# Five neighbouring rows on a partition for wq, w1, x and gate_w, and w2's tile zeroed in eight pieces behind the gate

## The chip, the cores and the metric

The kernel runs on one core of a Trainium2 chip. The metric is the time of one execution in device microseconds (us). Lower is better. The core has a matrix engine (PE), a vector engine (DVE), a scalar engine (ACT), GpSimd (POOL) and a synchronisation engine (SP) that here only issues transfers. Sixteen DMA engines move data between device memory and the on-chip memory, which has 128 partitions.

## The reference

The kernel computes the output of a gated mix of two branches for one token (one row x of 640 values), and the gradients of nine inputs. Branch A is attention over a cache of 32 heads, 4096 positions and 128 features a head. Branch B is a dense layer with the Mish activation. All tensors are bf16.

```python
# x: [1,1,640]; k_cache, v_cache: [1,32,4096,128]; wq: [640,4096]; wo: [4096,640]
# w1: [640,1728]; b1: [1728]; w2: [1728,640]; gate_w: [640]
q = (x @ wq).reshape(1, 1, 32, 128).transpose(0, 2, 1, 3)
p = softmax(einsum("bhqd,bhkd->bhqk", q, k_cache) * 128 ** -0.5)
a = einsum("bhqk,bhkd->bhqd", p, v_cache).transpose(0, 2, 1, 3).reshape(1, 1, 4096) @ wo
h = x @ w1 + b1
b = (h * tanh(softplus(h))) @ w2
g = sigmoid((x * gate_w).sum(-1, keepdims=True))
out = g * a + (1 - g) * b
# returned: out and the gradients for x, k_cache, v_cache, wq, wo, w1, b1, w2, gate_w
```

The two caches are 33.6 MB each and are read once. Their gradients are as large and are written once. wq, wo, w1 and w2 (5.2, 5.2, 2.2 and 2.2 MB) are read once, and so are their gradients written. That is 164 MB of traffic in all. Each gradient of a weight is an outer product (the gradient of wq is x times a row), and so is the gradient of each cache head.

## The kernel before, in words

**Heads.** The loop at L758 takes one head after another. A head's K and V tile are [128 partitions, 32 positions, 128 features] with 8192 contiguous bytes on a partition. PE transposes them (L530) and ACT copies the transposed pieces out of PE's accumulators (L539); PE forms the rows of scores (L553), a short chain of DVE, PE and ACT does the softmax (L576 to L608), and DVE writes the two outer products (L613) into a buffer of four (`o_sb`), from which SP stores them (L631). `dv_out` and `dk_out` are these two, and in the last heads they write into the K and V buffers instead. Four K and four V buffers are loaded ahead: behind a head's first store SP issues the loads of the head four later (L809, L810, issuing at L106 and L111).

**Groups.** Four heads make a group. A group needs its slice of wq for the queries (`g_q`, L230) and a tile of wo (transposed at L343) for the gradient that enters each head (`g_do`, L282). wq is loaded for two groups at once (`load_wqp`, L123) into a tile [128, 5, 1024]. When a group is through, its slice of wq is overwritten in place by the gradient (`f_dwq`, L391) and the tile is stored (`f_dwq_st`, L396). The 640 rows of wq lie on 128 partitions, so each partition holds five rows: row r is on partition r mod 128.

**Branch B.** `w1_sb` is [128, 5, 1728] with the same order of rows, loaded at L148 as the last of the first loads; its gradient is written over it (L515) and stored by L822 and L823 in the last but one turn of the loop. `w2_sb` [128, 16, 640] is loaded by POOL through a list of row numbers (`w2_load`, L196, issued in head 0) that leaves 20 of the 128 partitions out; half the tile is set to zero before (L416). The pieces of branch B are worked off a list (`mq`), a few to a head.

**Vectors.** x, grad_out and gate_w come in as five rows of 128 each (L130 to L132, on ACT's queue), fifteen rows in one tile. PE transposes them in one go (L691), so that element c*128+p is on partition p, column c; `cols_bf` and `cols_f` hold the fifteen columns. The first matmul for the queries (L230) needs the columns and the first wq tile. At the end `fin` [128, 15] holds the output and the gradients of x and gate_w as columns; PE transposes it back (L934), ACT copies it (L936) and POOL stores three times five rows (L937 to L939).

**Gate.** z is the sum of x*gate_w, and `g_raw` (L713) the sigmoid of it; `g_all` and `omg_all` scale grad_out for the two branches (L729, L730, L732).

**Order.** Each engine works through its instructions in the order in which they are written; there is no planner. SP's queue holds nearly all the transfers: the first loads (K0, wq, wo, V0, K1, V1, K2, wo, V2, K3, V3, w1), then the stores and loads of each head. ACT's queue holds four small loads at the start, and POOL's the loads of b1 (L418), small moves for branch B, the two transfers of w2 and the last stores. POOL's first work is the identity (L155, L156), small memsets (L209 to L214), the memset of h_sb (L415) and that of w2's half tile (L416), then the loads of b1. DVE's first work is built from the identity; `ident_f` (L165) is what PE's first transposes wait for.

Of the kernel before, what the change touches and what calls it, by code (L numbers as in the profile page):

```python
# [10 lines left out]
F32 = mybir.dt.float32  # L11
BF16 = mybir.dt.bfloat16
# [4 lines left out]
def kernel(  # L17
# [24 lines left out]
    nc = tc.nc  # L42
    P = 128
    _, H, Sk, Dh = A_k_cache.shape
    D = A_x.shape[-1]
# [3 lines left out]
    RC = D // P  # L49
    G = 4  # L50
    NG = H // G
    GD = G * Dh
    FCN = 16
# [14 lines left out]
    dVv = out_3.rearrange("b h (p j) d -> (b h) p j d", p=P)  # L68
    wq_v = A_wq.rearrange("(rc r) c -> r rc c", r=P)
    dwq_v = out_4.rearrange("(rc r) c -> r rc c", r=P)  # L70
    wo4_v = A_wo.rearrange("(g p t) n -> g p t n", p=P, t=4)
    dwo4_v = out_5.rearrange("(g p t) n -> g p t n", p=P, t=4)
    assert G == 4 and NG % 2 == 0
    w1_v = B_w1.rearrange("(rc r) f -> r rc f", r=P)
    dw1_v = out_6.rearrange("(rc r) f -> r rc f", r=P)
    w2_v = B_w2.rearrange("(i fc) n -> i (fc n)", fc=FCN)
    dw2_v = out_8.rearrange("(i fc) n -> i (fc n)", fc=FCN)
    b1_v = B_b1.rearrange("(i fc) -> i fc", fc=FCN)
    db1_row = out_7.rearrange("(o f) -> o f", o=1)
    x_rows = A_x.rearrange("a b (c p) -> (a b c) p", p=P)  # L80
    dy_row = grad_out.rearrange("a b d -> (a b) d")
    dy_rows = grad_out.rearrange("a b (c p) -> (a b c) p", p=P)
    gw_rows = gate_w.rearrange("(c p) -> c p", p=P)
    out0_rows = out_0.rearrange("a b (c p) -> (a b c) p", p=P)
    out1_rows = out_1.rearrange("a b (c p) -> (a b c) p", p=P)
    out9_rows = out_9.rearrange("(c p) -> c p", p=P)

# [40 lines left out]

    vec_rows = const.tile([3 * RC, P], BF16, name="vec_rows")
    nc.scalar.dma_start(vec_rows[0:RC, :], x_rows)  # L130
    nc.scalar.dma_start(vec_rows[RC:2 * RC, :], dy_rows)
    nc.scalar.dma_start(vec_rows[2 * RC:3 * RC, :], gw_rows)  # L132
    mjunk = const.tile([P, F], BF16, name="mjunk")
# [13 lines left out]
    w1_sb = const.tile([P, RC, F], BF16, name="w1_sb")  # L147
    nc.sync.dma_start(w1_sb[:], w1_v)  # L148
    w2_sb = const.tile([P, FCN, D], BF16, name="w2_sb")
# [25 lines left out]
    def grp(shape, dt, name):  # L175
        return grp_ps.tile(shape, dt, name=name, tag="grp")
# [82 lines left out]
    def g_qcol(g):  # L259
        groups[g]["col"] = col_mm(groups[g]["q_row"])  # L260
# [154 lines left out]
    nc.gpsimd.memset(h_sb[:], 0.0)  # L415
    nc.gpsimd.memset(w2_flat[0:P // 2, :].bitcast(F32), 0.0)  # L416
    for a, b, i in SEG:
# [340 lines left out]
    for h in range(H - 1):  # L758
# [211 lines left out]
```

## Time and profile before

| | |
|---|---|
| median of 3 runs | 401.1 us (400.16 to 402.86) |
| the profiled execution | 400.45 us, span 398.5 us, granted PE clock 0.912 |
| PE, DVE, ACT, POOL busy | 305.1, 294.4, 232.8, 18.6 us |
| DMA queue of SP | 159.62 MB in 27312 packets, 96.5% of sixteen engines' span |
| DMA queue of POOL | 4.44 MB in 672 packets, 2.8% |
| moved in all | 164.55 MB, 413 GB/s over the span |

The span runs from the first to the last instruction of the profiled execution; the execution's own time has 1.95 us around it. An engine's busy time is the time in which it worked on an instruction. The DMA share is the mean busy share of the sixteen DMA engines; as packets overlap a little in the records, it can go somewhat over 1. A packet is one contiguous piece that a DMA engine moves.

### The profile page before, as it was taken

How to read it: one execution, taken by the hardware profiler on the slowest of the kernel's cores; microseconds unless marked ns; L12 is line 12 of the kernel's file. 1: busy time of each engine (PE TensorE's matmuls, PEld its weight loads, DVE VectorE, ACT ScalarE, POOL GpSimd, SP SyncE). 2: the span in 40 equal slices, each digit the busy share in tenths (PEclk: the TensorE clock that was granted, in tenths of full speed). 3: DMA queues.
4: the chain of work that ended last, by engine and by line, in shares of the span. 5: the costliest groups of instructions: out<-in, count | busy, mean ns of one | idle time of the engine just before them, and what ended most of it. 6: DMA issues, size and time to landing. Idle time of an engine off the chain costs nothing.

```text
span 398.5 us, 7712 instructions
## 1 busy us (share of the span) xinstructions
PE 305.1 (77%) x2933; PEld 206.1 (52%) x2949; DVE 294.4 (74%) x819; ACT 232.8 (58%) x468; POOL 18.6 (5%) x34
## 2 busy tenths in 40 slices
PE   2979979697898985885888977968797988677540
PEld 1556637464556663553565645645465645455320
DVE  8217728769696875778898986687898986669790
ACT  2466746654667663763566778575678756375320
POOL 8001010000000000000000030000000000010001
PEclk9999999968998998999898999879899899889855
DMA  7999999999999999999999999999999999999996
GB/s 271 424 416 409 401 425 421 424 420 424 423 426 424 422 417 423 426 415 427 424 423 425 422 424 421 426 412 423 427 423 426 423 424 421 423 435 404 406 417 251
DMA packets 28052, 164.55 MB, mean 413 GB/s; under 512 B 2967, under 2 KB 2968, under 8 KB 11416
## 3 DMA queue, kind: packets, MB, share of 16 engines
q1 hardware_dynamic: 27312, 159.62, 96.5%
q0 software_dynamic: 672, 4.44, 2.8%
q8 instruction: 23, 0.38, 0.4%
q14 instruction: 13, 0.11, 0.1%
q10 hardware_dynamic: 32, 0.01, 0.0%
HBM read 82.44 MB, written 82.44 MB: 414 GB/s over the span
## 4 chain that ended last, share of the span: by engine, by line
DMA 46%; DVE 28%; PE 17%; ACT 5%; issue 2%; POOL 0%; POOLq 0%; DVEq 0%; ACTq 0%
DMA out_dram<-o_sb 44%; DVE o_sb L613 10%; PE tr L530 7%; DVE junk L381 4%; DMA out_dram<-Vn 2%; DVE wq_p L391 2%; PE rw L553 2%; PE rw L646 2%; DVE mjunk L510 1%; DVE ident_f L165 1%; PE do_ps L282 1%; ACT do_row L285 1%; DVE Vn L613 1%; PE x L570 1%; ACT rw_sb L564 1%
## 5 line engine op out<-in xcount | busy, mean ns | idle before, releaser
L539 ACT COPY T<-tr 128x512 f32<-128x512 f32 x256 | 137.9, 595 | 54.6 <-PE tr L530 36.6
L613 DVE TENSOR_TENSOR o_sb<-qs_row,ds 128x2048 bf16<-128x2048 bf16 x58 | 70.7, 1218 | 35.5 <-DMA out_dram<-o_sb 35.5
L530 PE MATMUL tr<-ident_f,Vn 128*128 128x128 f32 x512 | 87.3, 306 | 6.8 <-ACT T L539 6.1
L530 PE MATMUL tr<-ident_f,Kn 128*128 128x128 f32 x512 | 85.7, 295 | 7.3 <-DVE ident_f L165 7.3
L530 PEld LDWEIGHTS tr<-ident_f,Vn 128*128 128x128 f32 x512 | 65.3, 158 | 27.9 <-PE tr L530 12.7
L530 PEld LDWEIGHTS tr<-ident_f,Kn 128*128 128x128 f32 x512 | 61.6, 150 | 23.8 <-PE rw L646 13.5
L613 DVE TENSOR_TENSOR o_sb<-do_row,p 128x2048 bf16<-128x2048 bf16 x58 | 69.8, 1246 | 0.0
L564 ACT COPY rw_sb<-rw 128x512 f32<-128x512 f32 x33 | 19.3, 586 | 49.1 <-PE rw L553 47.6
L646 PE MATMUL rw<-Kn,ds 128*4 128x512 bf16 x256 | 36.7, 413 | 3.5 <-DVE ds L608 3.2
L646 PE MATMUL rw<-Vn,p 128*4 128x512 bf16 x256 | 36.7, 413 | 0.0
L582 PE MATMUL mx<-ident_f,m_s 128*128 128x128 f32 x32 | 10.4, 325 | 27.5 <-DVE m_s L578 27.4
L570 PE MATMUL x<-ident_f,rw_sb 128*128 128x128 f32 x132 | 22.1, 291 | 4.6 <-ACT rw_sb L564 1.4
L381 DVE SCALAR_TENSOR_TENSOR junk<-wq_p,dq_bc 128x512 bf16<-128x512 bf16 x35 | 23.9, 684 | 0.0
L553 PE MATMUL rw<-T,qz 128*32 128x512 bf16 x256 | 22.5, 429 | 0.0
L598 PE MATMUL mx<-zd,ones_f 128*128 128x2 f32 x64 | 10.9, 241 | 14.2 <-DVE pj L594 14.0
L399 ACT ACTIVATE wo_g<-da_bc,o 128x640 bf16<-128x640 bf16 x28 | 20.9, 818 | 1.0 <-PE ax_ps L369 1.0
L553 PE MATMUL rw<-T,doz 128*32 128x512 bf16 x256 | 20.7, 400 | 0.8 <-ACT T L539 0.8
L590 ACT ACTIVATE e_bf<-x,negM 128x32 bf16<-128x32 f32 x32 | 9.4, 292 | 20.5 <-DVE dqo L654 20.3
L570 PEld LDWEIGHTS x<-ident_f,rw_sb 128*128 128x128 f32 x132 | 14.1, 143 | 13.5 <-ACT rw_sb L564 13.5
L582 PEld LDWEIGHTS mx<-ident_f,m_s 128*128 128x128 f32 x32 | 4.5, 141 | 32.0 <-DVE m_s L578 31.9
L646 PEld LDWEIGHTS <-ds 128*4 128x4 bf16 x256 | 9.3, 87 | 19.9 <-DVE ds L608 8.2
L598 PEld LDWEIGHTS mx<-zd,ones_f 128*128 128x128 f32 x64 | 10.5, 207 | 17.2 <-DVE pj L594 14.6
(177 smaller groups left out, 381.9 us busy)
## 6 DMA issues: line engine op xcount, KB each, us to landing
out_dram<-o_sb SPq DMA_DIRECT2D x58, 1024.0 KB, 16.2
Kn<-in_A_k_cache_dram SPq DMA_DIRECT2D x32, 1024.0 KB, 16.1
Vn<-in_A_v_cache_dram SPq DMA_DIRECT2D x32, 1024.0 KB, 17.7
wq_p<-in_A_wq_dram SPq DMA_DIRECT2D x4, 1280.0 KB, 14.2
wo_g<-in_A_wo_dram SPq DMA_DIRECT2D x8, 640.0 KB, 17.0
out_dram<-wo_g SPq DMA_DIRECT2D x8, 640.0 KB, 16.4
out_dram<-wq_p SPq DMA_DIRECT2D x4, 1280.0 KB, 10.9
out_dram<-Kn SPq DMA_DIRECT2D x3, 1024.0 KB, 10.0
```

The lines of the kernel that those rows point to most:

```text
L381: nc.vector.scalar_tensor_tensor(jq[:], in0=wqs[g][:, c, :], scalar=1.0, in1=groups[g]["dq_bc"][:], op0=ALU.mult, op1=ALU.mult, accum_out= ...
L399: nc.scalar.activation(wos[g][:, hh, :], da_bc[:], ACT.Copy, scale=groups[g]["o4"][:, hh:hh + 1])
L530: nc.tensor.transpose(tp[:, t, :], words[:, t * P:(t + 1) * P], ident_f[:])
L539: nc.scalar.copy(T[h][:, (3 - c) * (TB // 2):(4 - c) * (TB // 2), :], tp[:])
L553: nc.tensor.matmul(rw[32 * c:32 * (c + 1), :], lhsT=z[:, par, :, :].rearrange("p m u -> p (m u)"), rhs=Tb[:, c, par, :, :], start=first an ...
L564: nc.scalar.copy(rw_sb[h][:].rearrange("p t r -> p (t r)"), rw[:])
L570: nc.tensor.transpose(xs[h][:, 3 - j, :], t[:, j, :], ident_f[:])
L582: nc.tensor.transpose(mx[:, 0:P], dgms.pop(h)[:].to_broadcast([P, P]), ident_f[:])
L590: nc.scalar.activation(es[h][:], sd[h][0], ACT.Exp, bias=negM[:], scale=scale, accum_out=zds[h][:, 0:1])
L598: nc.tensor.matmul(mx[:, P:P + 2], lhsT=ones_f[:], rhs=zds[h][:], start=True, stop=True)
L613: nc.vector.tensor_tensor(dst[:, a:b, :].rearrange("p j (k t) -> p j k t", t=4), row.rearrange("p (k t) -> p k t", t=4).unsqueeze(1).to_br ...
L646: nc.tensor.matmul(rw[32 * c:32 * c + 4, :], lhsT=c4[:, 4 * jb:4 * jb + 16].rearrange("p (j t) -> p t j", t=4)[:, 0, :], rhs=N[:, jb:jb + ...
```

## The change

wq, w1, x, gate_w and their gradients are laid out so that partition p holds rows 5p to 5p+4. For w1 and its gradient the five rows of a partition are then one contiguous piece of 17280 bytes instead of five of 3456, and the gradient is stored in one transfer instead of two. For wq the pieces stay at 2048 bytes, since only 1024 of the 4096 columns are moved at a time. x and gate_w are loaded straight into columns, ten bytes on a partition; only grad_out is still transposed. The gradients of x and gate_w are stored straight from the columns, before the output is transposed back. grad_out, the output, wo and w2 keep their order.

The memset of w2's half tile is cut into eight of [64, 1280] bf16 and moved behind the gate; a POOL copy of `g_raw` into a spare place makes POOL wait for it.

```diff
-    wq_v = A_wq.rearrange("(rc r) c -> r rc c", r=P)
-    dwq_v = out_4.rearrange("(rc r) c -> r rc c", r=P)
+    wq_v = A_wq.rearrange("(r rc) c -> r rc c", r=P)
+    dwq_v = out_4.rearrange("(r rc) c -> r rc c", r=P)
...
-    w1_v = B_w1.rearrange("(rc r) f -> r rc f", r=P)
-    dw1_v = out_6.rearrange("(rc r) f -> r rc f", r=P)
+    w1_v = B_w1.rearrange("(r rc) f -> r (rc f)", r=P)
+    dw1_v = out_6.rearrange("(r rc) f -> r (rc f)", r=P)
...
-    x_rows = A_x.rearrange("a b (c p) -> (a b c) p", p=P)
+    x_v = A_x.rearrange("a b (p c) -> (a b p) c", p=P)
...
-    vec_rows = const.tile([3 * RC, P], BF16, name="vec_rows")
-    nc.scalar.dma_start(vec_rows[0:RC, :], x_rows)
-    nc.scalar.dma_start(vec_rows[RC:2 * RC, :], dy_rows)
-    nc.scalar.dma_start(vec_rows[2 * RC:3 * RC, :], gw_rows)
+    cols_bf = const.tile([P, 3 * RC], BF16, name="cols_bf")
+    vec_rows = const.tile([RC, P], BF16, name="vec_rows")
+    nc.scalar.dma_start(cols_bf[:, 0:RC], x_v)
+    nc.scalar.dma_start(vec_rows[:], dy_rows)
+    nc.scalar.dma_start(cols_bf[:, 2 * RC:3 * RC], gw_v)
...
-    nc.sync.dma_start(w1_sb[:], w1_v)
+    nc.sync.dma_start(w1_sb[:].rearrange("p c f -> p (c f)"), w1_v)
...
-    nc.gpsimd.memset(w2_flat[0:P // 2, :].bitcast(F32), 0.0)
...
-    cols_ps = grp([P, 3 * RC], BF16, "cols_ps")
-    nc.tensor.transpose(cols_ps[:], vec_rows[:], ident_bf[0:3 * RC, 0:3 * RC])
-    cols_bf = const.tile([P, 3 * RC], BF16, name="cols_bf")
-    nc.vector.tensor_copy(cols_bf[:], cols_ps[:])
+    cols_ps = grp([P, RC], BF16, "cols_ps")
+    nc.tensor.transpose(cols_ps[:], vec_rows[:], ident_bf[0:RC, 0:RC])
+    nc.vector.tensor_copy(cols_bf[:, RC:2 * RC], cols_ps[:])
...
     nc.vector.reciprocal(g_raw[:], en[:])
+    nc.gpsimd.tensor_copy(dx_parts[:, 0, NG + 2:NG + 3], g_raw[:])
+    for fc in range(0, FCN, 2):
+        nc.gpsimd.memset(w2_flat[0:P // 2, fc * D:(fc + 2) * D].bitcast(F32), 0.0)
...
-            nc.sync.dma_start(dw1_v[:, 0:3, :], w1_sb[:, 0:3, :])
-            nc.sync.dma_start(dw1_v[:, 3:RC, :], w1_sb[:, 3:RC, :])
+            nc.sync.dma_start(dw1_v, w1_sb[:].rearrange("p c f -> p (c f)"))
...
-    fin_ps = grp([3 * RC, P], BF16, "fin_ps")
-    nc.tensor.transpose(fin_ps[:], fin_bf[:], ident_bf[:])
-    fin_rows = vec_rows
-    nc.scalar.copy(fin_rows[:], fin_ps[:])
-    nc.gpsimd.dma_start(out0_rows, fin_rows[0:RC, :])
-    nc.gpsimd.dma_start(out1_rows, fin_rows[RC:2 * RC, :])
-    nc.gpsimd.dma_start(out9_rows, fin_rows[2 * RC:3 * RC, :])
+    nc.gpsimd.dma_start(out1_v, fin_bf[:, RC:2 * RC])
+    nc.gpsimd.dma_start(out9_v, fin_bf[:, 2 * RC:3 * RC])
+    fin_ps = grp([RC, P], BF16, "fin_ps")
+    nc.tensor.transpose(fin_ps[:], fin_bf[:, 0:RC], ident_bf[:])
+    nc.scalar.copy(vec_rows[:], fin_ps[:])
+    nc.gpsimd.dma_start(out0_rows, vec_rows[:])
```

In the instructions as built, the device-memory side of each wq transfer becomes one list of 640 rows of 1024 elements, because neighbouring rows follow each other at one distance; before it was 128 by 5 by 1024, as the on-chip side is in both kernels. For w1 both sides are 128 by 8640. All engines' instructions keep their order but for POOL's and the last stores.

More of the change, by code (lines that the diff above doesn't have):

```diff
@@ L79 @@
     db1_row = out_7.rearrange("(o f) -> o f", o=1)
-    x_rows = A_x.rearrange("a b (c p) -> (a b c) p", p=P)
+    x_v = A_x.rearrange("a b (p c) -> (a b p) c", p=P)
     dy_row = grad_out.rearrange("a b d -> (a b) d")
     dy_rows = grad_out.rearrange("a b (c p) -> (a b c) p", p=P)
-    gw_rows = gate_w.rearrange("(c p) -> c p", p=P)
+    gw_v = gate_w.rearrange("(p c) -> p c", p=P)
     out0_rows = out_0.rearrange("a b (c p) -> (a b c) p", p=P)
-    out1_rows = out_1.rearrange("a b (c p) -> (a b c) p", p=P)
-    out9_rows = out_9.rearrange("(c p) -> c p", p=P)
+    out1_v = out_1.rearrange("a b (p c) -> (a b p) c", p=P)
+    out9_v = out_9.rearrange("(p c) -> p c", p=P)
     const = ctx.enter_context(tc.tile_pool(name="const", bufs=1))
```

## Prediction

> **What bounds the kernel now.** I read the page's queues first, then the span cut into single microseconds at its start and end, then who SP waited for, then the first instructions in order of time.
>
> The page, busy shares in forty slices and the queues:
>
> ```profile
> PE   2979979697898985885888977968797988677540
> DVE  8217728769696875778898986687898986669790
> DMA  7999999999999999999999999999999999999996
> ...
> q1 hardware_dynamic: 27312, 159.62, 96.5%
> q0 software_dynamic: 672, 4.44, 2.8%
> ```
>
> The reader is to see that the DMA row has a 9 in every slice but the first and the last, while no engine does. The queues together fill sixteen engines' span to 99%. So the time is the time of the packets, plus what is lost at the two ends. The records of the single packets in the trace give what a packet takes (medians): 2048 B 84 ns, 3456 B 135 ns, 5120 B 196 ns, 8192 B 309 ns, 20480 B 761 ns. All lie on 8.5 ns + 36.8 ns per 1000 B within 1.5 ns. Sixteen engines at 8192 B in 309 ns move 424 GB/s, which is what the middle slices of the page show.
>
> The ends, from the busy times by single microseconds (after the engines' columns: PE clock, DMA share, GB/s):
>
> ```profile
> 5.00:6.00 1.00, 0.00 (x0) 0.00 (x0) 1.00 (x3) 0.00 (x0) 1.00 (x1) 1.00 0.94 332
> 6.00:7.00 1.00, 0.00 (x0) 0.00 (x0) 1.00 (x3) 0.00 (x0) 1.00 (x1) 1.00 1.02 306
> 7.00:8.00 1.00, 0.72 (x4) 0.73 (x5) 0.97 (x10) 0.00 (x0) 1.00 (x3) 1.00 0.96 268
> ...
> 37.00:38.00 1.00, 1.00 (x14) 0.69 (x6) 0.07 (x2) 0.60 (x2) 0.00 (x0) 1.00 0.89 369
> ...
> 39.00:40.00 1.00, 1.00 (x18) 0.41 (x20) 1.00 (x2) 0.45 (x1) 0.00 (x0) 1.00 0.81 332
> ```
>
> ```profile
> 392.00:393.00 1.00, 0.00 (x0) 0.00 (x0) 0.00 (x0) 0.00 (x0) 0.00 (x0) 0.50 0.97 376
> 393.00:394.00 1.00, 0.00 (x0) 0.00 (x0) 0.00 (x0) 0.00 (x0) 0.00 (x0) 0.50 0.56 214
> 394.00:395.00 1.00, 0.00 (x0) 0.00 (x0) 0.00 (x0) 0.00 (x0) 0.00 (x0) 0.50 0.54 206
> ```
>
> From 5 to 8 us the DMA engines are busy but move 268 to 332 GB/s: that is the first wq tile. Its 640 packets average 102.7 ns; those of the other seven wq transfers average 85.1. At 37 to 40 us, between the last first load and the first stores, about 0.3 us is empty (0.11 and 0.19). From 393 us on only half the DMA engines still work, for 3.5 us, on the last store (wo's gradient). All engines had computed by then: the last busy instructions before it are the issues of the last small stores, at 390.7 us.
>
> Who SP waited for in the first 15 us, and DVE and PE in order of time:
>
> ```profile
> SPq L111 <- DMA Kn<-in_A_k_cache_dram: 2.2, 1, 2.2
> SPq L106 <- DMA wq_p<-in_A_wq_dram: 2.1, 1, 2.1
> ```
>
> ```profile
> 1.75 5.47 DVE L165 CAST ident_f<-ident_bf 128x128 f32<-128x128 bf16 x1
> ```
>
> The second of these fences is shown for its 5.47 us: a copy of 128x128 that ran as long as POOL's memsets (the small ones, then w2's half tile, 2.78 to 7.13 us). PE's first transposes wait for it until 7.28. SP's waits date two landings: K0 at 5.71 us (SP goes on issuing then) and wq at 9.98 us. The first matmul for the queries starts at 10.00, so it is wq's landing that starts the chain of head 0, not the late identity.
>
> **The change part by part.**
>
> *w1 and its gradient.* Each way, five packets of 135 ns a partition become one of 17280 B: by the line above 8.5 + 636 = 644 ns instead of 675, 31 ns saved. A DMA engine has 8 of 128 partitions, so 0.25 us each way and **-0.5 us** on a bound resource. If the 17280 bytes were cut again, the saving shrinks towards nothing; POOL's w2 packets go whole at 20480 B, so I take it in full. One store issue instead of two (0.60 and 1.26 us of SP at 371.8 us) frees SP, which next waits 3.0 us for DVE anyway: nothing.
>
> *x, gate_w and their gradients.* Fifteen packets each way shrink to five, and 256 of 10 B are added each way: 16 an engine. The trace has 32 B packets at 9 ns, 4 B at 9 and 216 B stores at 16. At 10 ns it is 0.16 us an engine each way, **+0.3 us**; the ends are 0.2 and 0.5. Landing: the small loads share the engines with K0 and wq, and even the last of them now (1280 B, moved at 6.8 us) is ahead of wq's landing at 9.98; sixteen more small packets in turn with wq's 84 ns ones add 1.5 us. Covered by wq. Without that cover it would cost these 1.5 us at head 0 only.
>
> *The last stores.* POOL issues two of three straight from `fin_bf` (ready at 388.25) and the third behind them: three times 0.5 us ends at 389.9 instead of 390.7. What ends last is wo's gradient, issued at 386.2, which landed 11.3 us later at 397.5; SP was through with the small stores at 395.9. Their 1.6 us of room covers the ten-byte stores; price if it doesn't: the excess over 1.6. I take **0**.
>
> *The memset out of the front.* `ident_f` no longer waits for 4.35 us of memset. PE can start at K0's landing, 5.7 instead of 7.28, but still meets wq at 9.98: gain 0 if wq lands as before. The first wq tile and K0 are slow in just the time of that memset (640 packets with 17.6 ns over the others is 0.7 us an engine). Whether they are slow for that reason the trace can't tell: between 0 and -0.7, and I take **-0.3**. b1's three loads move forward by 4 us on POOL, to where nothing waits for them until head 2.
>
> *The memset behind the gate.* `g_raw` is ready at 13.38. POOL's copy and eight memsets (4.35 us by the row of the whole) fill it to about 18 us. Behind them on POOL is only w2's load, which waited for row numbers until 32.3: hidden by 14 us. DVE beside it is rival B.
>
> *wq.* As many packets of 2048 B as before: **0**, unless rival A.
>
> Sum: -0.5 + 0.3 - 0.3 = **-0.5 us**. The profiled execution took 400.45 us, so 399.95; it lies 0.65 below the median of the runs, so against that median the forecast is 401.1 - 0.5 = **400.6 us**.
>
> **A rule on ports.** The CAST above began at 1.75 us, and six of POOL's small memsets ended between then and 2.78 without letting it go; it ended 0.09 us after the last memset. The Trainium skill ("SBUF — State Buffer", SBUF: two separate sides) says that VectorE's two-port modes and GpSimd share one port pair as a lock, held "for the whole instruction". By the Trainium skill a memset cut in eight lets VectorE in after 0.54 us (4.35/8), an estimate; in this trace the ends of instructions did not let it in. The Trainium skill would make rival B cost at most 0.5 us; the row gives the price below.
>
> **The rivals.**
>
> *A: the wq transfers get slower (slower).* The change makes the device side of the eight wq transfers one list of 640 rows against 128 partitions by 5. If the sixteen engines then share out the tile otherwise than the other tiles, engines meet at the same partitions and packets take longer. For it: w2's load, the one transfer with its own list of rows, averaged 860.5 ns a packet against 761, with single ones at 1601. Against it: 640 and 128 divide by sixteen alike, and the first wq tile was slow with the old list too. Price: 8 x 40 = 320 packets an engine on a bound resource. At +13% (w2's load) 3.5 us, at +17.6 ns (the first wq tile against the others) 5.6 us, doubled (w2's worst) 27 us. I take the wq row, as it is the same tile: 400.6 + 5.6 = **406.2 us**. It decides against "no change" when a wq packet averages over 99 ns (85.1 + 4.5 us/320). The Trainium skill ("DMA: Bandwidth & Descriptors", Why a DMA increments its semaphore by 16 and not by 1) takes the number of engines from the largest divisor up to 16 of both outermost sizes, which is 16 here; on which partitions each engine gets then, it speaks only for the 128-partition case. No run here shows it yet.
>
> *B: the memset moves its stall to the gate.* If DVE stands from 13.4 to 18.0 us as it did at 1.75 to 7.2, the work from `g_bf` to the halves of `da_bc` (13.97 to 15.6) comes 4.0 us late. ACT's `db_bc` follows, and behind it the copies for `wT` that `do_ps` needs (18.6 to 19.85); with ACT's 0.99 + 1.06 + 1.40 us from 19.1 on, that ends at 22.6, about 2.9 us late. The first store, issued at 33.65, moves to 36.5, its packets to 37.6, while w1's last ends at 36.6: 1.0 us empty, on top of the 0.3 already there. w2's load is late with it. 400.6 + 1.0 = **401.6 us**, at most 403. Against it: the DVE instructions there read PSUM or have one column; the reductions at 1.35 and 1.55 us (0.29 and 0.28 us) ran beside POOL's memsets.
>
> *C: the start does shift.* If wq lands 0.7 us earlier and x's columns, ready before it, leave PE nothing to do first, head 0 is 0.7 to 1.5 us earlier and the empty 0.3 us goes: 400.6 - 1.3 = **399.3 us**. Against more: DMA is full from 3 us on, and an earlier store only queues.
>
> **How the numbers follow.** Forecast 0.50, A 0.28, B 0.12, C 0.10. Half of A's prices lie under 409, few of C's under 398, so 398 to 409 leaves out about 0.16. A measurement tells about 1%, 4 us, from no change. Slower by more than that: 0.25 of A and 0.02 of B, 0.27. Faster by more: 0.04 of C and 0.01 of the rest, 0.05. Within: 0.68.
>
> **What would show it.** In the changed kernel's packets: 256 of 17280 B at some 644 ns; wq's 2048 B at 84 to 85 ns (over 99: A). DVE's `ident_f` at 0.3 us or so; the first matmul of the queries at 9.3 to 10 us; no DVE instruction of over 1 us between 13 and 18 (else B); the first store at 33 to 34 us. Last landing still wo's gradient. I am wrong if the ten-byte stores land last, if wq's packets grow, or if the half of the DMA engines that ends late ends much later.

## The result and the profile after

| | before | after |
|---|---|---|
| median | 401.28 us (6 runs, 400.16 to 402.86) | 404.47 us (6 runs, 403.73 to 406.06) |
| ratio | | 1.0084, 95% interval 1.0056 to 1.0112 |
| the profiled execution | 400.45 us, span 398.5 | 406.05 us, span 403.9 |

The change makes the kernel slower by 0.84%, some 3.4 us; the forecast was 0.5 us faster. (A ratio here is the estimate from all runs of a comparison, not exactly the quotient of the two medians.) The two profiled executions lie further apart than the medians, 5.6 us; the reason for that comes out below.

The page of the kernel after, the rows shown of before:

```profile
PE   2879979887898985975887977968897977777630
DVE  3406646878696875797897985687898986679770
DMA  7997999999999999999999999999999999999995
...
q1 hardware_dynamic: 26272, 159.62, 95.3%
q0 software_dynamic: 672, 4.44, 3.0%
```

The DMA row now has a 7 in its fourth slice, 30.3 to 40.4 us, which was a 9. The packets themselves need no more time: SP's queue took 95.3% of 403.9 us, 384.9 us of sixteen engines, and 96.5% of 398.5 us before, 384.6 us. The loss is empty time, at the start and at the end.

Six instructions in the order of time in the kernel after (start, length, engine and line; in brackets what was waited for):

```profile
1.75 1.17 DVE L166 CAST ident_f<-ident_bf 128x128 f32<-128x128 bf16 x1
11.29 2.29 PE L231 MATMUL q_ps<-wq_p,cols_bf 128*128 128x512 bf16 x5 [3.03 <-DMA wq_p<-in_A_wq_dram]
14.86 4.63 POOL L715 MEMSET w_sb<- 64x640 f32 x8
16.80 2.71 DVE L734 TENSOR_SCALAR da_col<-cols_f,g_all 128x5 bf16<-128x5 f32 x1
37.12 0.35 SPq L631 DMA_DIRECT2D out_dram<-o_sb  x1
391.80 0.18 DVE L933 CAST fin_bf<-fin 128x15 bf16<-128x15 f32 x1
```

And the four of before that are compared with them (`ident_f` of before stands with the prediction):

```profile
10.00 2.29 PE L230 MATMUL q_ps<-wq_p,cols_bf 128*128 128x512 bf16 x5 [0.64 <-DVE zj L705]
15.52 0.22 DVE L732 TENSOR_SCALAR da_col<-cols_f,g_all 128x5 bf16<-128x5 f32 x1
33.65 0.35 SPq L631 DMA_DIRECT2D out_dram<-o_sb  x1
388.07 0.18 DVE L932 CAST fin_bf<-fin 128x15 bf16<-128x15 f32 x1
```

The queries start 1.29 us later, the first store 3.47 us, and the last copy, 354.4 us after the first store before and 354.7 after it now, 3.73 us. From that copy to the end of the span it was 10.4 us and is 12.1.

So there are three things to explain: the late queries, the still later first store, and the longer end. The windows show the last two. At the start of the stores, and at the end (columns after the engines: PE clock, DMA share, GB/s):

```profile
33.00:34.00 1.00, 0.96 (x9) 0.87 (x10) 0.29 (x2) 0.96 (x2) 0.00 (x0) 1.00 0.89 380
34.00:35.00 1.00, 1.00 (x12) 0.63 (x13) 0.88 (x5) 1.00 (x3) 0.00 (x0) 1.00 0.49 207
35.00:36.00 1.00, 1.00 (x24) 0.40 (x16) 1.00 (x2) 0.10 (x1) 0.27 (x1) 1.00 0.31 129
36.00:37.00 1.00, 0.89 (x12) 0.42 (x5) 1.00 (x1) 0.64 (x2) 0.92 (x1) 1.00 0.04 17
37.00:38.00 1.00, 1.00 (x8) 0.85 (x8) 1.00 (x2) 0.93 (x2) 0.00 (x0) 1.00 0.90 193
38.00:39.00 1.00, 0.52 (x5) 0.43 (x5) 0.55 (x4) 0.58 (x1) 0.00 (x0) 1.00 0.59 168
...
397.00:398.00 1.00, 0.00 (x0) 0.00 (x0) 0.00 (x0) 0.00 (x0) 0.00 (x0) 0.50 0.62 154
398.00:399.00 1.00, 0.00 (x0) 0.00 (x0) 0.00 (x0) 0.00 (x0) 0.00 (x0) 0.50 0.62 62
399.00:400.00 1.00, 0.00 (x0) 0.00 (x0) 0.00 (x0) 0.00 (x0) 0.00 (x0) 0.50 0.40 37
```

From 33 to 39 us the shares sum to 3.22 of 6: the first loads are through, the first store has not come, and 2.8 us are lost. From 397 to 400 us the engines are half busy, as they were at the end before (0.54 to 0.56), but move 37 to 154 GB/s where they moved 206 to 214.

The issues of the last transfers after 386 us, before (the last column is the time from issue to landing):

```profile
out_dram<-wo_g SPq DMA_DIRECT2D x1, 640.0 KB, 11.3
out_dram<-vec_rows POOLq DMA_DIRECT2D x3, 1.2 KB, 5.7
```

and after:

```profile
out_dram<-wo_g SPq DMA_DIRECT2D x1, 640.0 KB, 12.9
out_dram<-fin_bf POOLq DMA_DIRECT2D x2, 1.2 KB, 8.3
out_dram<-vec_rows POOLq DMA_DIRECT2D x1, 1.2 KB, 8.0
```

wo's gradient, no part of the change, takes 1.6 us longer to land, and the 1.2 KB of row stores behind the ten-byte ones 8.0 us where it took 5.7.

### The profile page after: what moved, and what is told of

Read it like the earlier page. It is cut to its first block, busy times and chain, and to the rows that moved or that the text cites. A ratio compares the mean times of both kernels' runs of the same rounds, so it can differ in the third digit from the quotient of the medians.

```text
span 403.9 us, 7721 instructions
## 1 busy us (share of the span) xinstructions
PE 307.2 (76%) x2933; PEld 208.4 (52%) x2949; DVE 292.5 (72%) x819; ACT 233.2 (58%) x468; POOL 19.2 (5%) x42
## 3 DMA queue, kind: packets, MB, share of 16 engines
q1 hardware_dynamic: 26272, 159.62, 95.3%
## 4 chain that ended last, share of the span: by engine, by line
DMA 47%; DVE 29%; PE 16%; ACT 4%; issue 2%; POOL 0%; POOLq 0%; SPq 0%; DVEq 0%; ACTq 0%
DMA out_dram<-o_sb 44%; DVE o_sb L613 11%; PE tr L530 6%; DVE junk L382 4%; DMA wq_p<-in_A_wq_dram 2%; DVE wq_p L392 2%; PE rw L553 2%; PE rw L646 2%; DVE junk L489 1%; DVE Vn L613 1%; PE do_ps L283 1%; DVE mjunk L510 1%; ACT do_row L286 1%; ACT rw_sb L564 1%; DVE Kn L613 1%
## 5 line engine op out<-in xcount | busy, mean ns | idle before, releaser
L530 PE MATMUL tr<-ident_f,Vn 128*128 128x128 f32 x512 | 88.9, 311 | 7.8 <-ACT T L539 7.2
L530 PEld LDWEIGHTS tr<-ident_f,Vn 128*128 128x128 f32 x512 | 67.3, 161 | 28.7 <-PE tr L530 12.9
L582 PE MATMUL mx<-ident_f,m_s 128*128 128x128 f32 x32 | 10.4, 324 | 27.2 <-DVE m_s L578 27.2
## 6 DMA issues: line engine op xcount, KB each, us to landing
out_dram<-Kn SPq DMA_DIRECT2D x3, 1024.0 KB, 10.2
```

Of the source, the lines that this page charges most:

```text
L530: nc.tensor.transpose(tp[:, t, :], words[:, t * P:(t + 1) * P], ident_f[:])
L582: nc.tensor.transpose(mx[:, 0:P], dgms.pop(h)[:].to_broadcast([P, P]), ident_f[:])
```

## The experiments

Fifteen kernels were run: twelve are one part of the change alone, the change without one part, or a variant of such a part, and three (e8, e11, e12) try what should cover or remove the losses found. All were timed against the kernel before on their own chip; where two of them are compared, the chips may differ, and the ratios carry that. The numbers first, one profile each; "GB/s" is what the DMA engines moved from 33 to 43 us, "clock" the granted PE clock from 20 to 29 us, "tail" the time from the last copy (`fin_bf`) to the end of the span.

| kernel | ratio [95%] | queries | clock | first store | GB/s | `fin_bf` | tail |
|---|---|---|---|---|---|---|---|
| before | | 10.00 | 1.00 | 33.65 | 402 | 388.07 | 10.4 |
| after | 1.0084 [1.0056, 1.0112] | 11.29 | 0.81 | 37.12 | 246 | 391.80 | 12.1 |
| e1 memset behind the gate | 0.9999 [0.9981, 1.0017] | 10.11 | 1.00 | 33.82 | 392 | 388.46 | 10.0 |
| e2 after, memset in front | 1.0078 [1.0051, 1.0106] | 11.09 | 1.00 | 35.12 | 330 | 389.67 | 12.5 |
| e3 ten-byte stores | 1.0055 [1.0031, 1.0078] | 9.87 | 0.81 | 35.87 | 312 | 390.62 | 12.2 |
| e4 after, row stores | 1.0032 [1.0006, 1.0058] | 10.51 | 0.81 | 36.39 | 278 | 391.10 | 9.9 |
| e5 wq | 1.0039 [1.0016, 1.0061] | 11.25 | 1.00 | 34.80 | 350 | 389.37 | 10.3 |
| e6 ten-byte loads | 1.0012 [0.9992, 1.0033] | 9.80 | 1.00 | 33.40 | 411 | 387.79 | 10.1 |
| e7 w1 | 0.9992 [0.9973, 1.0011] | 9.93 | 0.81 | 35.86 | 294 | 390.74 | 9.5 |
| e8 before, w2 earlier | 0.9966 [0.9949, 0.9983] | 9.79 | 0.81 | 35.73 | 414 | 388.55 | 9.2 |
| e9 wq as 4 + 1 rows | 1.0039 [1.0021, 1.0057] | 10.31 | 0.81 | 36.13 | 300 | 390.76 | 10.2 |
| e10 one ten-byte store | 1.0041 [1.0016, 1.0066] | 10.15 | 0.81 | 36.07 | 307 | 390.85 | 11.6 |
| e11 after, w2 earlier | 1.0030 [1.0009, 1.0051] | 12.02 | 0.82 | 37.89 | 388 | 390.85 | 11.0 |
| e12 after with three edits | 0.9995 [0.9972, 1.0018] | 12.01 | 0.81 | 37.77 | 396 | 390.04 | 10.0 |
| e13 wq, first tile in the old order | 1.0007 [0.9987, 1.0027] | 10.12 | 1.00 | 34.21 | 376 | 388.95 | 9.9 |
| e14 ten-byte stores, ACT's queue | 1.0051 [1.0029, 1.0073] | 10.03 | 0.81 | 35.90 | 311 | 390.77 | 11.9 |
| e15 ten-byte stores, one engine | 1.0107 [1.0080, 1.0135] | 10.07 | 1.00 | 33.87 | 399 | 388.40 | 15.1 |

**Three sums in this table.** From the queries to the first store it is 23.55 to 24.09 us in all profiles with a clock of 1.00, and 25.76 to 26.00 in all with 0.81 or 0.82. From the first store to `fin_bf` it is 354.4 to 354.9 us wherever w2 is loaded in head 0, and 352.3 to 353.0 in the three with w2 earlier (e8, e11, e12). So, with w2 loaded in head 0, whatever makes the first store late shifts the rest of the execution rigidly. And the bytes say that this lateness is lost transfer time: before, 4.02 MB move from 33 to 43 us, and after 2.46, which is 1.56 MB less, 3.7 us at the 424 GB/s of the middle, for a first store 3.47 us later. So reckoned, e13 loses 0.6 us (0.56 later), e5 1.2 (1.15), e2 1.7 (1.47), e3 2.1 (2.22) and e4 2.9 (2.74); e6 gains 0.2 (0.25 earlier). Three things move the end: the landing of the first wq tile, the PE clock in head 0, and the tail. Which clock an execution meets isn't decided by the change: of the four kernels that differ from before in the last stores alone (e3, e10, e14, e15), three met 0.81 and one 1.00. Whether a later start changes how often the low clock is met, single profiles can't show, and a ratio would contain it. As a profile is one execution, causes are priced by the ratios, and the profiles show where the time lies.

### The memset alone, and the change without it (e1, e2)

e1 is the kernel before with the memset moved:

```diff
-    nc.gpsimd.memset(w2_flat[0:P // 2, :].bitcast(F32), 0.0)
...
     nc.vector.reciprocal(g_raw[:], en[:])
+    nc.gpsimd.tensor_copy(dx_parts[:, 0, NG + 2:NG + 3], g_raw[:])
+    for fc in range(0, FCN, 2):
+        nc.gpsimd.memset(w2_flat[0:P // 2, fc * D:(fc + 2) * D].bitcast(F32), 0.0)
```

> The kernel before with only one part of the change: w2's half tile is zeroed in eight pieces behind the gate. Theory S (the loss at the start comes from this move: PE starts early, pauses for wq, DVE stands beside the memsets, the first store comes late and the DMA engines run empty at 34 to 38 us): 1.5 to 3 us slower than before, one DVE instruction of over 2 us between 13 and 20 us, at least 1.5 us of empty DMA share between 33 and 40 us. Theory W (the loss at the start comes from wq's and x's loads, the move is harmless): within 0.5 us of before, first store at 33 to 34 us.

e2 is the kernel after with the memset back at its old place, in one piece:

```diff
     nc.gpsimd.memset(h_sb[:], 0.0)
+    nc.gpsimd.memset(w2_flat[0:P // 2, :].bitcast(F32), 0.0)
...
-    nc.gpsimd.tensor_copy(dx_parts[:, 0, NG + 2:NG + 3], g_raw[:])
-    for fc in range(0, FCN, 2):
-        nc.gpsimd.memset(w2_flat[0:P // 2, fc * D:(fc + 2) * D].bitcast(F32), 0.0)
```

> The changed kernel with the memset put back in one piece at the front. Theory S: 1.5 to 3 us faster than the changed kernel, so 0.3 to 1.7 us slower than before; first store at 33 to 35 us. Theory W: as slow as the changed kernel, 3 us over before.

e1 measured 0.9999, e2 1.0078 against the change's 1.0084: the place of the memset makes no difference either way. The instructions of e1 in the order of time:

```profile
13.68 4.64 POOL L715 MEMSET w_sb<- 64x640 f32 x8
15.63 2.71 DVE L734 TENSOR_SCALAR da_col<-cols_f,g_all 128x5 bf16<-128x5 f32 x1
33.82 0.35 SPq L630 DMA_DIRECT2D out_dram<-o_sb  x1
```

`da_col` is a product of 128x5 that took 0.22 us before and takes 2.71 here. It begins in the middle of the eight memsets and ends with them (15.63 + 2.71 = 18.34, 13.68 + 4.64 = 18.32), as it does in the kernel after (19.51 and 19.49). At 0.58 us a piece, at least four memsets ended without letting it go on. So the stall did move to the gate. It cost nothing that can be seen: the first to need `da_col` is `do_ps`, PE comes to it at 18.78 us (18.60 before), 0.44 us after `da_col` is done, and the first store goes out at 33.82 instead of 33.65. Other profiles agree: from the queries to `do_ps` it is 9.52 us in the kernel after and in e11, with the stall, and 9.52 in e3, e7 and e8, without it.

The Trainium skill ("SBUF — State Buffer", SBUF: two separate sides) has VectorE and GpSimd share a port pair by a lock held for one whole instruction, by which, so read, the wait would be at most one piece, 0.58 us. This trace disagrees: 2.71 us, over four ends of instructions.

### The ten-byte stores alone, and the change without them (e3, e4)

e3 is the kernel before with the last stores of the change:

```diff
-    fin_ps = grp([3 * RC, P], BF16, "fin_ps")
...
-    nc.gpsimd.dma_start(out1_rows, fin_rows[RC:2 * RC, :])
-    nc.gpsimd.dma_start(out9_rows, fin_rows[2 * RC:3 * RC, :])
+    nc.gpsimd.dma_start(out1_v, fin_bf[:, RC:2 * RC])
+    nc.gpsimd.dma_start(out9_v, fin_bf[:, 2 * RC:3 * RC])
+    fin_ps = grp([RC, P], BF16, "fin_ps")
...
```

> The kernel before with only the last stores changed: the gradients of x and gate_w go out straight from columns, ten bytes a partition, ahead of the output (their elements land in another order than the reference's, since the columns are still the old ones). Theory T (the ten-byte stores hold the DMA engines up at the end): 1.2 to 2.2 us slower than before, with 2 to 3 us at the end in which the engines are half busy and move under 160 GB/s, and packets of over 400 ns in the last stores. Rival H (hidden behind the last store of wo's gradient, as predicted): within 0.4 us of before.

e4 is the kernel after with the reverse of that edit.

> The changed kernel with the last stores as before: all three vectors transposed and stored as five rows each (the gradients of x and gate_w then land in another order than the reference's). Theory T: 1.2 to 2.2 us faster than the changed kernel, so 1 to 2 us slower than before. Rival H: as slow as the changed kernel.

e3 measured 1.0055, and e4 1.0032 where the whole change has 1.0084. Putting the ten-byte stores in costs 2.2 us, taking them out gives back 2.1 (0.0052 of 401.3). By the middle values it is the largest part. In e3, by single microseconds at its end:

```profile
396.00:397.00 1.00, 0.00 (x0) 0.00 (x0) 0.00 (x0) 0.00 (x0) 0.00 (x0) 0.50 0.93 153
397.00:398.00 1.00, 0.00 (x0) 0.00 (x0) 0.00 (x0) 0.00 (x0) 0.00 (x0) 0.50 0.28 42
398.00:399.00 1.00, 0.00 (x0) 0.00 (x0) 0.00 (x0) 0.00 (x0) 0.00 (x0) 0.50 0.58 50
```

The engines are up to 93% busy and move 42 to 153 GB/s. The records of the packets say whose time that is. The ten-byte pieces show as 32 packets of 80 B on POOL's queue, of 22 ns on average in e3 and 32 in the kernel after: short. The packets of the transfers beside them have grown: the last wq gradient averages 105.1 ns a packet (before: 85.0), and in the kernel after wo's gradient averages 242 ns with single packets of 1800 (before: 203, at most 241).

### How many, from which queue, and through how many engines (e10, e14, e15)

Three variants of e3. In e10 only gate_w's gradient goes in ten-byte pieces. In e14 both go out from ACT's queue instead of POOL's. In e15 they go out from ACT's queue as 127 and 1 partitions each, so that they don't divide among the sixteen engines.

```diff
-    nc.gpsimd.dma_start(out1_v, fin_bf[:, RC:2 * RC])
-    nc.gpsimd.dma_start(out9_v, fin_bf[:, 2 * RC:3 * RC])
+    for t, o in ((1, out1_v), (2, out9_v)):
+        nc.scalar.dma_start(o[0:P - 1, :], fin_bf[0:P - 1, t * RC:(t + 1) * RC])
+        nc.scalar.dma_start(o[P - 1:P, :], fin_bf[P - 1:P, t * RC:(t + 1) * RC])
```

> The kernel before with only gate_w's gradient stored in ten-byte pieces (its elements land in another order than the reference's). If each such transfer costs its own time: half of what two cost, 0.7 to 1.3 us slower than before, the span ends 11.0 to 11.4 us after the last conversion instead of 10.4 (none) or 12.2 (two). If the first already costs all, because its pieces hold up the same engines: 1.8 us or more.

> The kernel before with the two gradients stored in ten-byte pieces as in the run of the small stores alone, but issued from ACT's queue instead of POOL's (elements in another order than the reference's). If the pieces themselves hold the DMA engines up: 1.5 to 2.2 us slower than before, span end 11.9 to 12.5 us after the last conversion. If POOL's queue does (its 80-byte packets of eight pieces): under 0.7 us slower.

> As the previous kernel, but each of the two stores split in one of 127 partitions and one of the last, which leaves the transfer to one DMA engine instead of sixteen (fewer 4-byte completion packets show it). If pieces of neighbouring partitions from several engines meet in the same place of device memory: span end 10.2 to 11.0 us after the last conversion, under 0.7 us slower than before. If each piece is slow by itself: one engine has 127 of them in a row, span end over 13 us after, 2 us or more slower.

e10 measured 1.0041 with a tail of 11.6 us, between its two forecasts, e14 1.0051 with 11.9, e15 1.0107 with 15.1. So the queue doesn't matter, half the pieces cost 1.6 us where all cost 2.2 (their intervals overlap), and one engine alone makes it worse. e15 at its end:

```profile
393.00:394.00 1.00, 0.00 (x0) 0.00 (x0) 0.00 (x0) 0.08 (x1) 0.53 (x1) 0.50 1.21 101
394.00:395.00 1.00, 0.00 (x0) 0.00 (x0) 0.00 (x0) 0.00 (x0) 0.00 (x0) 0.50 0.72 20
395.00:396.00 1.00, 0.00 (x0) 0.00 (x0) 0.00 (x0) 0.00 (x0) 0.00 (x0) 0.50 0.39 48
```

At 394 us the engines are 72% busy and move 20 GB/s. That one engine does the small pieces is read from the packets: the four transfers leave four 4-byte packets on ACT's queue, where e14's two leave 32, and at most two ten-byte packets are under way at once, where e14 has up to eight. Meanwhile the packets of wo's gradient take 392 ns on average for 5120 B. So the cause isn't that several engines meet at one place with their small pieces. The records don't name a packet's engine, but an engine or two with small pieces can't be the 72% that are busy: large writes of other engines are held up, hence the thing held up is shared; what it is, no run here shows. Some of e15's larger cost may come from its pieces going out 2.6 us earlier than e14's (391.8 and 394.4 us), beside more of wq's gradient.

The Trainium skill ("DMA: Bandwidth & Descriptors", Specifications) puts the smallest transfer at full rate at 512 B and says that below it the engine reads, modifies and writes. No run here shows the reading and writing, and the size written alone doesn't explain the low rates (20 to 153 GB/s in the windows above). e12 (below) stores both gradients as 32 pieces of 80 B, and the kernel before its last rows as 15 pieces of 256 B: both are under 512 B, with tails of 10.0 and 10.4 us and no packet of wo's gradient over 259 ns. In e12 less of the large stores was left when the pieces went out (some 0.2 MB, 0.6 in e3), and they were read from one partition, not as ten bytes from each of 128; which of the two matters isn't separated.

### wq alone (e5), and what of it (e9, e13)

e5 is the kernel before with wq's rows, and those of its gradient, in the new order:

```diff
-    wq_v = A_wq.rearrange("(rc r) c -> r rc c", r=P)
-    dwq_v = out_4.rearrange("(rc r) c -> r rc c", r=P)
+    wq_v = A_wq.rearrange("(r rc) c -> r rc c", r=P)
+    dwq_v = out_4.rearrange("(r rc) c -> r rc c", r=P)
```

> The kernel before with only wq and its gradient in the new order of rows (x and w1 keep the old order, so the values of what depends on wq are not the reference's; the same number of bytes, packets and instructions). Theory L (the list of 640 rows makes the first wq tile land later): the first matmul of the queries at 10.5 to 11.3 us instead of 10.0, 0.5 to 1.5 us slower than before. Rival X (the ten-byte loads of x and gate_w, in turn with K0 and wq, make it land later): first matmul at 9.9 to 10.1 us, within 0.5 us of before. Both: wq packets at 84 to 86 ns after the first tile.

e5 measured 1.0039, 1.6 us. Its first queries and first store, then the same of e13, which is e5 with its first tile alone loaded in the old order:

```profile
11.25 2.29 PE L230 MATMUL q_ps<-wq_p,cols_bf 128*128 128x512 bf16 x5 [1.88 <-DMA wq_p<-in_A_wq_dram]
34.80 0.35 SPq L631 DMA_DIRECT2D out_dram<-o_sb  x1
```

```profile
10.12 2.29 PE L231 MATMUL q_ps<-wq_p,cols_bf 128*128 128x512 bf16 x5 [0.76 <-DMA wq_p<-in_A_wq_dram]
34.21 0.34 SPq L632 DMA_DIRECT2D out_dram<-o_sb  x1
```

```diff
-        nc.sync.dma_start(wqp[k][:], wq_v[:, :, a * GD:z * GD])
+        nc.sync.dma_start(wqp[k][:], (wq_old if k == 0 else wq_v)[:, :, a * GD:z * GD])
```

> As the kernel with only wq in the new order, but the first of its four tiles is loaded in the old order; the other three loads and all four stores are in the new one (the values of what depends on wq are not the reference's). If the new order costs only by the late first tile: first matmul of the queries at 9.8 to 10.2 us, within 0.5 us of before. If it costs in the later transfers: 1 to 1.6 us slower than before, as with all tiles in the new order.

e13 measured 1.0007 [0.9987, 1.0027]. The seven other wq transfers (three loads and the four stores of the gradient) are in the new order there, at 84 to 86 ns a packet, and cost nothing that can be told. So what e5 loses lies in the first tile, as far as the two ratios can tell, whose intervals just overlap. The second tile, loaded at 75 to 80 us, averages 87 to 90 ns in five of the seven profiles with every tile in the new order, which is 0.1 to 0.2 us an engine at 40 packets each.

In the records, the last packet of that tile ends at 9.39 to 9.74 us in all ten profiles with the old order, and at 10.20 to 11.68 in all seven with the new one (after, e2, e4, e5, e9, e11, e12). It isn't a tile of slower packets: they average 94 to 102 ns, and 92 to 103 in the old order. A few packets are late. From 9.75 us on, at most five of the tile are under way at once, and the longest after 9 us take 364 to 487 ns (at most 238 in the old order). As sixteen engines share the tile, this reads as a few engines being behind; the records don't name them.

e9 asks whether the list of 640 rows is to blame. It has the new order, but each tile is loaded as four rows of a partition and one row, whose device side can't be folded into one list:

```diff
-        nc.sync.dma_start(wqp[k][:], wq_v[:, :, a * GD:z * GD])
+        nc.sync.dma_start(wqp[k][:, 0:4, :], wq_v[:, 0:4, a * GD:z * GD])
+        nc.sync.dma_start(wqp[k][:, 4, :], wq_v[:, 4, a * GD:z * GD])
```

> As the kernel with only wq in the new order, but each wq tile is loaded by two transfers, one of four of a partition's five rows and one of the fifth, so that the device side is 128 by 4 by 1024 and 128 by 1024 instead of one list of 640 rows; the same rows on the same partitions and the same 2048-byte packets (the stores stay one list; the values of what depends on wq are not the reference's). If the list is the cause of the late first tile: first matmul of the queries at 9.8 to 10.2 us, within 0.5 us of before. If the order of the addresses is: at 11 us or later, 1 to 1.6 us slower than before.

It measured 1.0039 like e5. The queries start at 10.31 us there, between the two forecasts, since PE can begin with four rows, but the tile's last packet ends at 10.89. So the late packets don't need the list. Its 1.6 us are another matter: by the profile the queries are only 0.31 us later than before, and the first store, at 36.13, 0.1 to 0.3 us later than in the other profiles with the low clock, the old order and w2 in head 0 (e3, e7, e10, e14). None of its twelve runs lies near 400 us, where 14 of the 35 runs of before beside them lie under 400.6; it may have met the low clock more often, which no run shows. Why the new addresses leave a few packets late at the first load, and hardly at the later ones, stays open; that the first tile shares its time with K0 and the small loads is one difference.

### The ten-byte loads and w1 alone (e6, e7)

In e6, x and gate_w are loaded as columns and stored by rows; in e7, w1 and its gradient alone are laid the new way.

```diff
+    nc.scalar.dma_start(cols_bf[:, 0:RC], x_v)
+    nc.scalar.dma_start(cols_bf[:, 2 * RC:3 * RC], gw_v)
```

> The kernel before with only x and gate_w loaded as ten bytes a partition (wq and w1 keep the old order of rows, so the values of what depends on them are not the reference's). Theory L: first matmul of the queries at 9.9 to 10.1 us, within 0.5 us of before. Rival X: first matmul at 10.5 to 11.3 us, 0.5 to 1.5 us slower than before.

```diff
-    w1_v = B_w1.rearrange("(rc r) f -> r rc f", r=P)
-    dw1_v = out_6.rearrange("(rc r) f -> r rc f", r=P)
+    w1_v = B_w1.rearrange("(r rc) f -> r (rc f)", r=P)
+    dw1_v = out_6.rearrange("(r rc) f -> r (rc f)", r=P)
```

> The kernel before with only w1 and its gradient in the new order, one piece of 17280 bytes a partition (x keeps the old order, so the values of what depends on w1 are not the reference's). The prediction's term: 256 packets of 644 ns, 0.5 us faster than before. Rival: the larger packets end unevenly at the first stores and at the end, 0 to 1 us slower.

e6 measured 1.0012 [0.9992, 1.0033], e7 0.9992 [0.9973, 1.0011]: neither can be told from nothing. In e6 the queries start at 9.80 us, so wq isn't held up. In the packets of the kernel after, w1's pieces of 17280 B take 644 ns (median), as worked out ahead; -0.5 us would be 0.9988, inside the interval of e7.

### What covers a late first store: w2 earlier (e8, e11)

By the table every tenth of a microsecond that the first store comes later than 33.65 us is bytes not moved from 33 to 43 us. If that is because the first loads end there, one more load at that place should cover it. w2's 2.2 MB wait for their row numbers in the turn of head 0 and are issued at about the time of the first stores; e8 is the kernel before with both, row numbers and load, right behind the gate:

```diff
     nc.vector.tensor_scalar(da_col[:], dy_col_f, g_all[:], None, ALU.mult)
+    row_ids()
+    w2_load()
...
-        if h == 0:
-            row_ids()
-            w2_load()
```

> The kernel before with w2's load issued by POOL behind the gate's work (at 16 us) instead of in head 0 (at 32 us); nothing else. Theory K (the time goes up one for one with the first store once it is later than 33.7 us, because the first loads then run out): the empty DMA share between 33 and 40 us goes and the time no longer depends on the first store; 0.5 to 1.5 us faster than the median of before, and the spread of single runs is under 1.5 us. Rival R (the shift is passed on by the engines' order, not by empty DMA engines): as before, with the same spread of 2.5 us.

e11 is the kernel after with the same edit.

> The changed kernel with w2's load issued behind the gate's memsets (at 20 us) instead of in head 0. If the loss is the late first store plus the ten-byte stores: the first goes and the second stays, so 400.2 (the kernel before with the same move) + 2.0 - 0.5 (w1) = 401.7 us, 2.5 to 3 us faster than the changed kernel, single runs within 1.5 us of each other. If wq's list costs more than its first landing: 403 us or more.

e8 measured **0.9966 [0.9949, 0.9983]**, 400.13 us, and is the one kernel here that is faster than both. w2's issue, its first store, and the window from 33 to 43 us in its profile:

```profile
16.49 1.09 POOL L196 DMA_INDIRECT w_sb<-in_B_w_dram,rowids  x1 [7.67 <-DVE rowids L193]
35.73 0.35 SPq L631 DMA_DIRECT2D out_dram<-o_sb  x1
```

```profile
33.00:43.00 10.00, 9.43 (x103) 5.93 (x102) 8.35 (x17) 6.05 (x14) 0.00 (x0) 1.00 1.01 414
```

e3's first store is as late (35.87), with w2 at its old place:

```profile
20.00:29.00 9.00, 6.37 (x44) 4.63 (x44) 0.56 (x4) 4.80 (x7) 0.00 (x0) 0.81 1.01 420
33.00:43.00 10.00, 9.37 (x102) 5.87 (x102) 8.32 (x19) 5.99 (x14) 1.18 (x1) 1.00 0.87 312
```

e3 moves 312 GB/s there, e8 414, with first stores 0.14 us apart, and both met a clock of 0.81 from 20 to 29 us. e8's runs also lie closer together, 399.41 to 400.55, while those of before beside them go from 400.07 to 402.83. That fits an execution of before losing some 2 us whenever it meets the low clock, but the other runs have no windows to show it.

e11 measured 1.0030 [1.0009, 1.0051] where the change has 1.0084: the same edit takes 2.2 us off the kernel after and 1.4 off the kernel before; more was to be covered there, but the intervals don't tell the two gains apart. It is less than the 2.5 to 3 us expected. Part of what is left is the tail, 11.0 us.

### The change with three edits (e12)

e12 is the kernel after with the memset in front and w2 earlier, and with the gradients of x and gate_w put into one row each by twenty small matmuls (five to half a row), so that each is stored from one row of 1280 B (in the records 16 packets of 80 B).

```diff
+                nc.tensor.matmul(r_ps[:, :, c], lhsT=fin_bf[:, (v + 1) * RC + c:(v + 1) * RC + c + 1],
+                                 rhs=ident_bf[:, s * HP:(s + 1) * HP], start=True, stop=True)
...
+    nc.gpsimd.dma_start(out1_row, rows_sb[:, 0, :])
+    nc.gpsimd.dma_start(out9_row, rows_sb[:, 1, :])
```

> The changed layouts with w2's memset back at the front in one piece, w2's load behind the gate's work, and the gradients of x and gate_w turned into one row each by twenty small matmuls and stored in one piece each. If the two causes are all: 400.1 - 0.5 (w1) = 399.6 us, 1.5 us faster than before and 4.9 faster than the changed kernel. If the longer work at the end shows: the span ends over 11 us after the last conversion, and 400.5 us or more.

e12 measured 0.9995 [0.9972, 1.0018], not the 1.5 us faster that was expected. The tail is 10.0 us again. It isn't as fast as e8, and in its profile the queries come later still:

```profile
12.01 2.29 PE L231 MATMUL q_ps<-wq_p,cols_bf 128*128 128x512 bf16 x5 [2.64 <-DMA wq_p<-in_A_wq_dram]
37.77 0.35 SPq L632 DMA_DIRECT2D out_dram<-o_sb  x1
```

At 37.77 us the first store is somewhat past what even the earlier load covers (396 GB/s from 33 to 43 us, where e8 has 414). The two profiles with the latest queries, e11 and e12, are those with w2's load beside them at the start; whether it delays wq further isn't separated, as e8, with the old order, has its queries at 9.79.

### The sum

The single parts, as ratios above 1: memset -0.0001, stores 0.0055, wq 0.0039, loads 0.0012, w1 -0.0008, together 0.0097; the whole measured 0.0084 [0.0056, 0.0112]. The parts add up to it within the intervals, and nothing is left that needs the parts to act on each other.

In the two profiles: the queries 1.29 us later (wq), the way from there to the first store 2.18 us longer (with the low clock in head 0), the first store to `fin_bf` 0.26 us, the tail 1.7 us, in all 5.4, the difference of the spans. The 2.18 us is no property of the change, and is the reason why the profiles are further apart than the medians. From 20 to 29 us, before:

```profile
20.00:29.00 9.00, 6.59 (x63) 5.45 (x67) 1.31 (x8) 6.26 (x12) 0.00 (x0) 1.00 1.02 421
33.00:43.00 10.00, 9.28 (x98) 6.66 (x97) 8.21 (x18) 7.04 (x16) 0.44 (x1) 1.00 1.02 402
```

and after:

```profile
20.00:29.00 9.00, 6.64 (x45) 4.27 (x39) 0.43 (x3) 4.22 (x8) 0.00 (x0) 0.81 1.02 422
33.00:43.00 10.00, 9.33 (x93) 6.42 (x97) 7.60 (x20) 7.13 (x15) 1.19 (x1) 1.00 0.69 246
```

PE is busy as long (6.59 and 6.64 us), but for 45 instructions instead of 63, at a clock of 0.81 instead of 1.00; ten microseconds later the DMA engines move 246 GB/s instead of 402. Of the 2.18 us, 1.3 come behind `do_ps`, where this window lies, and 0.9 ahead of it: from the queries to `do_ps` it is 8.60 us before and 9.52 after, and twenty transposes of wo take PE 2.34 us where they took 1.82. The granted clock stands at 1.00 there in both. From the queries to `do_ps` it is 9.48 to 9.52 us in all ten profiles with the low clock, and 8.52 to 9.06 in the seven others. No run set the clock; that it is the cause is read from this agreement.

## Why the prediction was wrong

The measured 404.47 us lies in the range, 398 to 409, but on the other side of the kernel before than forecast, and for other causes than the one that made the range wide. That the range holds it is luck.

**What was right.** The bound (packets, plus the two ends), and with it the view that only the ends can matter; w1's 644 ns; the ten-byte loads hidden behind wq; `ident_f` free of the memset, 1.17 us instead of 5.47 (0.3 was forecast); the memset behind the gate at no cost; wo's gradient as the last to land.

**"The last stores. ... I take 0."** This step failed by the most: 2.2 us in e3. It priced the ten-byte pieces by their own packets (10 ns each, and those are short indeed) and gave them 1.6 us of room before wo's gradient lands. But the transfer that was to give the room is the one they hold up: it landed 12.9 us after its issue instead of 11.3. The rows drawn on gave what a small packet takes itself: 32 B and 4 B, and stored pieces of 216 B, sixteen in all (357.9 to 366.8 us), beside large stores. None was of ten-byte pieces, and none said what the packets beside them pay; the upper end should have been open there.

**"wq. As many packets of 2048 B as before: 0, unless rival A."** This failed by 1.6 us (e5). Rival A named the right part, but not the mechanism: over all eight transfers wq's packets average 89.4 ns in the kernel after and 87.3 before, under the 99 ns from which A decides, and the first tile's 98.4 against 102.7. The number that mattered wasn't a mean. The first tile's last packet is 0.5 to 2.3 us later, and the tile is done when its last packet is.

**The price of a late start (rivals B and C).** For B, 2.9 us of lateness was priced at 1.0 us of empty engines, and for C "an earlier store only queues". Neither holds. A first store 0.56 us later (e13) already costs 0.6 us of bytes, 3.47 us later (after) 3.7, and 0.25 us earlier (e6) brings 0.2. The kernel before has no cover left at its first store, and lateness passes through whole. The 0.3 us seen empty at 37 to 40 us was the sign of it, and was read as a small loss in itself. The DMA share also misled: in e5 it is 0.98 from 33 to 43 us at 350 GB/s, so engines that look busy moved 1.2 us less. By the right price B's 2.9 us would have been 2.9. B's own sum is off as well: ACT's last copy for `wT` ended at 18.78 us before, so an end at 22.6 is 3.8 us late, not 2.9.

**The memset out of the front: -0.3.** The gain didn't come: in e1 `ident_f` was 4.3 us shorter, and the first tile's last packet ended at 9.58 us, where it was 9.63. Its packets averaged 95.4 ns, inside the 92 to 103 of the profiles with the old order and the memset in front. So the memset wasn't why the first tile is slow.

**The memset behind the gate: 0, and rival B.** The 0 held although B's stall came: DVE stood for 2.71 us in `da_col`, which reads five columns of on-chip memory and which the argument against B ("read PSUM or have one column") had passed over. What failed in B is its path: the chain from `g_bf` to `da_bc` ran as before, only `da_col` stood, and it was done before PE came to the first matmul that needs it.

## What to carry to other kernels

Where the transfers are the bound, ask at both ends how long the work already queued lasts, and how late the first store can get before the engines run dry; a kernel at that edge pays for every later start in full, and one more load moved ahead of the edge (w2 here, 0.34%) is worth more than smoother packets. Price a store in pieces of a few bytes by what goes on beside it, not by its own packets, and keep it away from the last large transfers, as far as these runs go. When a layout changes what a first transfer reads, look at its last packet, not at the mean.

## What was not expected of the hardware

- 256 stored pieces of 10 B at the end of the kernel cost 2.2 us (e3), and all engines together move 37 GB/s in one microsecond of the kernel after; 128 pieces cost 1.6 us (e10), and 256 through one engine 4.3 us (e15), with 20 GB/s.
- Eight memsets of 0.58 us in a row held a DVE product of 0.22 us for 2.71 us (e1, after), over at least four ends of memsets.
- The same start of the kernel meets a PE clock of 1.00 or of 0.50 for 3.4 us near 24 us (0.81 from 20 to 29 us), and with the low clock the first store comes 2.2 us later: 33.65 before, 35.87 in e3.
- With its rows in the new order the first wq tile, of the same number of packets at the same mean, ends 0.5 to 2.3 us later through a few late packets (ten profiles against seven); later tiles hardly differ.
